# Writing out batch 0's TensorE queue by hand in a fused attention and SwiGLU kernel on one Trainium2 core

## The chip, the cores and the metric

The kernel runs on one core of one Trainium2 chip. The time is the device time of one execution in microseconds; with one core, this core's time is the kernel's. Times of a version are given as the median of its runs.

## What is computed

Attention over 8 batches of 12 heads, 448 positions and 64 numbers a head, and then a SwiGLU feed-forward block on the 3584 tokens. The weights are 768 x 1536 (gate and value) and 1536 x 768 (out).

```
scores = scale * np.matmul(q, k.transpose(0, 1, 3, 2))
attn = exp(scores - max) / (sum(exp) + 1e-9)
attn_out = np.matmul(attn, v)                     # (8, 12, 448, 64)
x = attn_out.transpose(0, 2, 1, 3).reshape(3584, 768)
g = x @ w_gate
silu = g * (1.0 / (1.0 + np.exp(-g)))
return (silu * (x @ w_val)) @ w_out               # (3584, 768), float32
```

## The kernel before

**Units of work.** Heads are worked in pairs: 48 pairs, 6 to a batch. Pairs below 12 (`QUAD`), the first two batches, keep their keys in chunks of 112, four to a pair. A *score tile* is one chunk of keys against all 448 queries of both heads: two matmuls into a tile of two PSUM banks (`qk`, line 287), followed by one exponential on ScalarE into `E` (line 301). `pv_chunk` (line 311) multiplies one chunk of `E` by V: eight matmuls of 65 columns into an accumulator, where column 64 gathers the sum of the exponentials. The fourth chunk is followed on VectorE by the reciprocal `R` and the product `xt` (lines 338 to 345). Pairs from 12 on use chunks of 128 keys, with a fourth, half chunk of two neighbouring pairs packed in one tile (`qk_quad`, line 257); their PV product is `pv_quad` (line 405), closed by `R` and `xt` for each head (lines 397 and 398).

**Turning.** Scores need q and k with the head's 64 numbers on the partitions (`qkT`). `prep` (line 199) makes them: pair 0 by matmuls with an identity (`turn0`), pairs 1 to 10 by TensorE transposes followed by one VectorE copy (`turn`, lines 243 to 253), pairs from 11 on by a reordering copy on POOL and a transposing DMA from SP (lines 188 to 197 and 211 to 221). The results `xt` are turned into `X`, the input of the feed-forward block, by `turn_x` (line 417): for pairs below 12 three matmuls and a VectorE cast (`X`, line 434), later by DMA. `turn_rests` (line 445) turns the last 64 queries of a batch's six pairs together.

**Feed-forward.** `ffn1_steps` (line 460) has 12 blocks of 128 hidden units. For each: a gate group of six matmuls into `gp`, a tanh on ScalarE (`sg`, line 480), a value group of six matmuls into `vp`, and two products on VectorE (`t`, line 484, and `hts`, line 487). `ffn2_steps` (line 492) multiplies the hidden units by `wo` in groups of 12 matmuls (`op`, line 510). In the first half-batch block a gate or value matmul has 384 columns.

**PSUM.** Two pools share the eight banks: `ps_s` has three tiles of two banks, given in rotation to score tiles, the early transposes and the gate groups; `ps_f` has two tiles of one bank, for accumulators, value groups, `op` and the other transposes.

**Order of the work.** Each engine works through its own queue in the order in which the program issues. Loads go through POOL's queue, in the order of the calls, except pair 0's; `load_v` brings V into `vraw`, and `copy_v` (line 167) copies it on VectorE into the tile `vo` that PV reads. `emit` issues the loads listed in `wq` when the score loop reaches a pair's second chunk. Batch 0 is the loop of lines 655 to 677: one score tile a turn, and between them, by conditions on the turn's number, the transposes of the coming pairs (`prep`), the V copies (`CAT`), the turned results (`XAT`), a few `dummy` matmuls and one or two PV chunks. From line 711 on a planner goes through `plan`: each visit `x` has two or three score tiles, and perhaps one or two pairs whose PV is due. A visit issues scores, the V copies for the next visit's pairs, loads and preps, PV, turned results, and then as many feed-forward steps as its budget allows. Visit 0 has the scores (6,0) and (6,1), the rest of batch 0's PV, the last two turned results and the first two feed-forward blocks.

The visit's head in the kernel before is this:

```
quads = [u for u in chunks if u[0] >= QUAD and u[1] == RU]
for pr, c in quads + [u for u in chunks if u not in quads]:
    qk(pr, c)
...
for p0 in vcopies.get(x, []):
    copy_v(p0)
```

Of the kernel before, what the change touches and what calls it, by code (L numbers as in the profile page):

```python
# [10 lines left out]
FP32 = mybir.dt.float32  # L11
FP16 = mybir.dt.float16
# [10 lines left out]
FIRST = 6  # L23
# [14 lines left out]
def kernel(  # L38
# [45 lines left out]
    xp = ctx.enter_context(tc.tile_pool(name="xp", bufs=2))  # L84
    hp_ = ctx.enter_context(tc.tile_pool(name="hp", bufs=2))
    fp = ctx.enter_context(tc.tile_pool(name="fp", bufs=3))
    ps_s = ctx.enter_context(tc.tile_pool(name="ps_s", bufs=3, space=PSUM))
    ps_f = ctx.enter_context(tc.tile_pool(name="ps_f", bufs=2, space=PSUM))

    Ebuf = [consts.tile([128, (NC * EB + 1) * D], FP16, name=f"E{i}") for i in range(NE)]  # L90
# [15 lines left out]

    wo = [consts.tile([128, NFB, OH], FP16, name=f"wo{i}") for i in range(2)]

    raw = {}
    qkT = {}  # L110
    X = {}

    def dummy(n):
        wp = ps_f.tile([128, 512], FP32, tag="f", name="wp")
# [84 lines left out]
    def prep(pr):  # L199
# [23 lines left out]

        def turn0():
            for t in range(2):
                tp = ps_s.tile([128, 2, 512], FP32, tag="s", name="tp")
                for c in range(NC):
                    for hx in range(2):
                        nc.tensor.matmul(
                            tp[ts(hx, 64), c // 2, ds(c % 2 * P, P)],  # L230
                            lhsT=qk16[:, 1 - t, c, hx],
                            rhs=ident[0:P, 0:P],
                            start=True,
                            stop=True,
                        )
                dst = qkT[pr][:, ts(1 - t, S)].rearrange("p (a x) -> p a x", a=2)
                nc.vector.tensor_copy(dst[:, 0], tp[:, 0, 0 : 2 * P])
                nc.scalar.activation(dst[:, 1], tp[:, 1, 0 : 2 * P], AF.Copy)
                if t == 0:
                    tq = tp  # L240
            nc.vector.tensor_copy(qkT[pr][:, 2 * S :], tq[:, 0, 0:D])

        def turn():
            if pr < FIRST + 2:
                tp = ps_s.tile([128, 2, 1024], FP16, tag="s", name="tp")[:, 0]
            else:
                tp = ps_f.tile([128, 1024], FP16, tag="f", name="tp")
            for i in range(2 * NC + 1):
                t, c = (1 - i // NC, i % NC) if i < 2 * NC else (0, 0)
                for hx in range(2):  # L250
                    src = raw[pr][t][:, hx, c, :]
                    nc.tensor.transpose(tp[ts(hx, 64), ts(i, P)], src, ident[0:P, 0:P])  # L252
            nc.vector.tensor_copy(qkT[pr][:], tp[:, 0 : 2 * S + D])
# [1 line left out]
        return turn if pr else turn0  # L255

    def qk_quad(pr, c):
        s = ps_s.tile([128, 2, 512], FP32, tag="s")
        if c < KR:
            t = qkT[pr]  # L260
            for hx in range(2):
# [25 lines left out]
    def qk(pr, c):  # L287
        if pr >= QUAD:
            return qk_quad(pr, c)
        t = qkT[pr]  # L290
        s = ps_s.tile([128, 2, 512], FP32, tag="s")
        for hx in range(2):
            nc.tensor.matmul(  # L293
                s[:, hx, 0:S],
                lhsT=t[ts(hx, 64), c * P : c * P + 128],
                rhs=t[ts(hx, 64), ds(S + (1 - hx) * D, S)],
                start=True,
                stop=True,
            )
        e = Es[pr % NE][:, ds(c * EB, 16)].rearrange("p (h b) x -> p h (b x)", h=2)  # L300
        nc.scalar.activation(e[:, :, 0:S], s[0:P, :, 0:S], AF.Exp, scale=sm_scale)  # L301
# [65 lines left out]
    def pv_open(pr):  # L367
        if pr not in accs:
            if wide(pr):
                acc = ps_s.tile([128, 2, 512], FP32, tag="s", name="acc")  # L370
                accs[pr] = ([acc[:, 0], acc[:, 1]], [0, 0], acc)
            else:
                accs[pr] = ([ps_f.tile([128, 512], FP32, tag="f", name="acc"), ps_f.tile([128, 512], FP32, tag="f", name="acc")], [0, 0])
# [69 lines left out]
        )  # L443

    def turn_rests(b):
        tp = ps_f.tile([128, NHP, D], FP32, tag="f", name="rtp")
        for p in range(NHP):
            for hx in range(2):
                nc.tensor.matmul(  # L449
# [7 lines left out]

    gate_small = [False]

    def ffn1_steps(kk, c0, n, hts):  # L460
        for fb in range(NFB):

            def group(kind, dst):
# [6 lines left out]
                        stop=(cb == NCB - 1),  # L470
                    )

            if gate_small[0]:
                gate_small[0] = False
                gp = ps_f.tile([128, 512], FP32, tag="f", name="gp")
            else:
                gp = ps_s.tile([128, 2, 512], FP32, tag="s", name="gp")[:, 0]
            group("g", gp)
            sg = fp.tile([128, 512], FP32, tag="sg")
            nc.scalar.activation(sg[:, 0:n], gp[:, 0:n], AF.Tanh, scale=0.5)  # L480
            vp = ps_f.tile([128, 512], FP32, tag="f", name="vp")
            group("v", vp)
            t1 = fp.tile([128, 512], FP32, tag="t1")
            nc.vector.scalar_tensor_tensor(  # L484
                t1[:, 0:n], sg[:, 0:n], 1.0, gp[:, 0:n], ALU.add, ALU.mult
# [1 line left out]
            nc.vector.scalar_tensor_tensor(  # L487
                hts[:, fb, 0:n], t1[:, 0:n], 0.5 * HS, vp[:, 0:n], ALU.mult, ALU.mult
            )
            yield  # L490

    def ffn2_steps(kk, c0, n, hts, first, last_block):
# [46 lines left out]
    def block(i):  # L539
        kk, odd = divmod(i, 2)  # L540
        c0, n = (384, 512) if odd else (0, 384)
        hts = hp_.tile([128, NFB, 512], FP16, tag="h")
        return ffn1_steps(kk, c0, n, hts), ffn2_steps(kk, c0, n, hts, i == 0, i == B - 1), n

    with tc.manual_schedule():
        load_qk32(0)
# [16 lines left out]
        dummy(7)  # L563
        prep(0)()
        dummy(1)
        turn = prep(1)

        wq = {
            0: [("qk", 6), ("g", 0), ("v", 0)],
# [75 lines left out]
        def share(total, at, n):  # L645
            return (at + 1) * total // n - at * total // n

        XAT = (11, 15, 17, 21)
        CAT = (4, 7, 11, 14, 17, 21)
        pieces = [(p, c) for p in range(FIRST) for c in range(NC)]  # L650

        def piece():
            pv_chunk(*pieces.pop(0))

        for u in range(FIRST * NC):
            pr, c = divmod(u, NC)
            qk(pr, c)
            if u == 1:
                dummy(1)
                turn()  # L660
                dummy(1)
            elif u == 3:
                dummy(2)
            elif u == 4:
                prep(2)()
            elif u >= 6 and c == 2:
                prep(pr + 2)()
            if c == 1:
                for w in wq.pop(pr, []):
                    emit(w)  # L670
            if u in CAT:
                copy_v(CAT.index(u))
            if u in XAT:
                turn_x(XAT.index(u))
            for _ in range(2 if c == 3 else int(c != 2 or u > 12)):
                if u >= 5 and pieces[0][0] * NC + pieces[0][1] <= u - 3:
                    piece()

        queue = []
        units = [divmod(x, NC) for x in range(QUAD * NC)]  # L680
# [30 lines left out]
        for x, (chunks, todo) in enumerate(plan):  # L711
            quads = [u for u in chunks if u[0] >= QUAD and u[1] == RU]
            for pr, c in quads + [u for u in chunks if u not in quads]:
                qk(pr, c)
            for _, p0 in todo:
                if p0 >= QUAD:
                    pv_piece(p0, RU)
            end = min([y for y in adds if y > x] + [len(plan) + 1])
            if x == 0:
                turn_x(4)  # L720
                while pieces:
                    piece()
                turn_x(5)
                add_block(0, end)
            for p0 in vcopies.get(x, []):
                copy_v(p0)
            entered = [pr for pr, c in chunks if c == 0]
            for pr in entered:
# [13 lines left out]
            for _, p0 in todo:  # L742
# [2 lines left out]
                    turns.append(p0)  # L745
                else:
                    turn_x(p0)
            for pr in entered:
                for w in wq.pop(pr, []):
                    emit(w)  # L750
            bare = not todo and bool(chunks)
            if adds[max(y for y in adds if y <= x)] < 2:
                if bare and oq and not fvq:
                    carry -= run_o()
# [60 lines left out]
```

The softmax here doesn't subtract the row's maximum and nothing guards it: scores larger than these inputs give would overflow.

## Time and profile before

| what | value |
| --- | --- |
| median of 5 runs | 452.09 us (450.84 to 452.89) |
| the profiled execution | 453.08 us, its span 451.3 us |
| TensorE matmuls busy | 439.3 us (97%) |
| TensorE weight loads busy | 247.1 us (55%) |
| ScalarE busy | 224.8 us (50%) |
| VectorE busy | 200.2 us (44%) |
| POOL busy | 180.2 us (40%) |
| gate and value matmuls (line 465) | 124.7 and 124.6 us |
| `op` matmuls (line 510) | 117.1 us |

PE stands for TensorE's matmuls, PEld for its weight loads, DVE for VectorE, ACT for ScalarE, POOL for GpSimd, SP for SyncE, whose queue issues the transposing DMAs. A line of the timeline gives start and duration in us, engine and line of the code, the operation with what it writes and reads, the shapes, and how many instructions are merged; in brackets the idle time before it and what ended it. Matmul ends are modelled and may overlap the next start. A line of the chain gives start, duration and what the time is put down to. A line of the windows view gives the stretch, its length, the busy time of PE, PEld, DVE, ACT and POOL, and last the granted share of TensorE's clock, the share of the DMA engines and GB/s.

### The profile page before, as it was taken

To read this page: it belongs to the slowest core of one execution; us is meant where nothing else is said; L and a number is where in the kernel's file an instruction comes from. 1 tells how busy PE (TensorE), PEld (TensorE's weight loads), DVE (VectorE), ACT (ScalarE), POOL (GpSimd) and SP (SyncE) were. 2 spreads that over 40 slices of the span, in tenths; PEclk is the share of its full clock that TensorE was granted. 3 is DMA by queue.
4 is the path that set the end of the run, shared out by engine and by line. 5 is a ranking of instruction groups with operands and counts; after the bars stand their busy time and mean duration, and the time that the engine had idled before them with its cause. 6 is when DMAs were issued, how large, how long until landed. Compare 5 with 4: busy or idle time off the path is not lost.

```text
span 451.3 us, 9959 instructions
## 1 busy us (share of the span) xinstructions
PE 439.3 (97%) x4024; PEld 247.1 (55%) x4024; DVE 200.2 (44%) x447; ACT 224.8 (50%) x332; POOL 180.2 (40%) x299
## 2 busy tenths in 40 slices
PE   7999999899999999999999999999999999999996
PEld 3656565444456556554556656554455656644464
DVE  4666563255565345344454535334544434045400
ACT  6965666456554555465536364455463651222222
POOL 8755716997775464335553267423000000000000
PEclk9999999899999999999999999999999999999999
DMA  9999999999997799984896687965131211200033
GB/s 143 176 200 201 198 179 148 151 219 159 130 137 89 116 140 125 143 102 66 110 122 104 107 136 99 152 78 103 32 78 47 48 45 22 77 30 1 0 107 105
DMA packets 108494, 49.90 MB, mean 111 GB/s; under 512 B 60832, under 2 KB 104992, under 8 KB 108448
## 3 DMA queue, kind: packets, MB, share of 16 engines
q0 software_dynamic: 46832, 24.56, 48.0%
q1 hardware_dynamic: 61520, 24.66, 29.4%
q8 instruction: 31, 0.51, 0.5%
q14 instruction: 15, 0.12, 0.1%
q10 hardware_dynamic: 96, 0.05, 0.0%
HBM read 49.55 MB, written 11.01 MB: 134 GB/s over the span
## 4 chain that ended last, share of the span: by engine, by line
PE 76%; DMA 12%; POOL 4%; DVE 3%; issue 2%; ACT 1%; DVEq 0%; POOLq 0%
PE op L510 23%; PE gp L465 22%; PE vp L465 19%; PE acc L356 8%; DMA k<-in_k_dram 5%; DMA wv<-in_moe_w_val_dram 4%; PE s L262 4%; DMA wg<-in_moe_w_gate_dram 2%; DVE t L484 1%; DVE hts L487 1%; ACT sg L480 1%; DMA vraw<-in_v_dram 1%; PE s L275 1%; POOL q L151 1%; POOL k L151 1%
## 5 line engine op out<-in xcount | busy, mean ns | idle before, releaser
L465 PE MATMUL gp<-X,wg 128*128 128x384 f16 (+1 forms) x576 | 124.7, 353 | 0.0
L465 PE MATMUL vp<-X,wv 128*128 128x384 f16 (+1 forms) x576 | 124.6, 352 | 0.0
L510 PE MATMUL op<-wo,hts 128*128 128x384 f16 (+1 forms) x684 | 117.1, 326 | 2.0 <-DVE xt L398 2.0
L283 ACT ACTIVATE E<-s 128x896 f16<-128x896 f32 x126 | 106.5, 922 | 14.4 <-PE s L262 9.2
L484 DVE SCALAR_TENSOR_TENSOR t<-sg,gp 128x384 f32<-128x384 f32 (+1 forms) x96 | 59.6, 621 | 119.5 <-ACT sg L480 119.5
L480 ACT ACTIVATE sg<-gp 128x384 f32<-128x384 f32 (+1 forms) x96 | 52.6, 548 | 92.9 <-PE gp L465 91.4
L510 PEld LDWEIGHTS <-hts 128*128 128x128 f16 x684 | 66.4, 99 | 48.2 <-issue 3.9
L465 PEld LDWEIGHTS <-wv 128*128 128x128 f16 x576 | 56.4, 98 | 52.6
L517 ACT ACTIVATE osb<-op 128x384 f32<-128x384 f32 (+1 forms) x57 | 27.6, 485 | 105.1 <-PE op L510 101.2
L465 PEld LDWEIGHTS <-wg 128*128 128x128 f16 x576 | 53.4, 98 | 45.5 <-issue 0.7
L487 DVE SCALAR_TENSOR_TENSOR hts<-t,vp 128x384 f16<-128x384 f32 (+1 forms) x96 | 59.6, 621 | 10.8 <-PE rtp L449 0.5
L188 POOL COPY qk<-k 128x512 f16<-128x512 f16 x36 | 22.8, 634 | 101.2 <-DMA qkT<-qk 99.1
L132 POOL DMA_DIRECT2D vraw<-in_v_dram x72 | 43.9, 631 | 14.6 <-DMA wo<-in_moe_w_out_dram 13.6
L356 PE MATMUL acc<-vo,E 128*128 128x65 f16 (+1 forms) x1152 | 43.1, 193 | 1.7 <-DVE hts L487 1.2
L301 ACT ACTIVATE E<-s 112x896 f16<-112x896 f32 x48 | 40.6, 916 | 7.9 <-PE s L293 7.8
L356 PEld LDWEIGHTS <-E 128*128 128x128 f16 (+1 forms) x1152 | 37.2, 96 | 13.1 <-issue 7.3
L132 POOL DMA_DIRECT2D k<-in_k_dram x70 | 42.4, 618 | 1.5 <-DMA wv<-in_moe_w_val_dram 0.8
L397 DVE RECIPROCAL R<-acc 128x4 f32<-128x4 f32 x68 | 12.1, 177 | 62.9 <-PE acc L356 62.9
L151 POOL DMA_DIRECT2D q<-in_q_dram x44 | 29.9, 680 | 4.8 <-PE tp L252 1.8
L398 DVE TENSOR_TENSOR xt<-acc,R 128x256 f16<-128x256 f32 x68 | 28.9, 424 | 2.3
L262 PE MATMUL s<-qkT 64*128 64x448 f16 x216 | 27.9, 353 | 0.0
L188 POOL COPY qk<-q 112x512 f16<-112x512 f16 x36 | 23.0, 640 | 0.0
(56 smaller groups left out, 184.4 us busy)
## 6 DMA issues: line engine op xcount, KB each, us to landing
vraw<-in_v_dram POOLq DMA_DIRECT2D x72, 64.0 KB, 4.7
q<-in_q_dram POOLq DMA_DIRECT2D x41, 112.0 KB, 3.6
k<-in_k_dram POOLq DMA_DIRECT2D x68, 64.0 KB, 4.5
wg<-in_moe_w_gate_dram POOLq DMA_DIRECT2D x8, 288.0 KB, 9.6
wv<-in_moe_w_val_dram POOLq DMA_DIRECT2D x8, 288.0 KB, 10.1
wo<-in_moe_w_out_dram POOLq DMA_DIRECT2D x2, 1152.0 KB, 19.9
out_dram<-osb SPq DMA_DIRECT2D x8, 288.0 KB, 4.1
out_dram<-osb SPq DMA_DIRECT2D x6, 336.0 KB, 2.9
```

Source lines behind the costliest of these rows:

```text
L132: eng.dma_start(dst[ts(s, 64)], rows)
L151: nc.gpsimd.dma_start(dst[0:P, ds(h0, 2 * n)], flat.rearrange("h (p c) d -> p h (c d)", c=NC))
L188: nc.gpsimd.tensor_copy(dst.rearrange("p c h d -> p h c d"), src)
L262: nc.tensor.matmul(s[:, hx, 0:S], lhsT=t[ts(hx, 64), ts(c + low(pr, hx), 128)], rhs=t[ts(hx, 64), ds(NC * 128, S)], start=True, stop=True,)
L283: nc.scalar.activation(e[:, 0 : 2 * S].rearrange("p (h q) -> p h q", h=2), s[:, :, 0:S], AF.Exp, scale=sm_scale)
L301: nc.scalar.activation(e[:, :, 0:S], s[0:P, :, 0:S], AF.Exp, scale=sm_scale)
L356: nc.tensor.matmul(accs[pr][0][hx][:, ts(j, D + 1)], lhsT=e[rows, ds(hx * S + j * 128, 128)], rhs=Vts[pr % NV][rows, hx, col, 0 : D + 1], ...
L465: nc.tensor.matmul(dst[:, 0:n], lhsT=wslice(kind, fb, cb), rhs=X[kk][:, cb, ds(c0, n)], start=(cb == 0), stop=(cb == NCB - 1),)
L480: nc.scalar.activation(sg[:, 0:n], gp[:, 0:n], AF.Tanh, scale=0.5)
L484: nc.vector.scalar_tensor_tensor(t1[:, 0:n], sg[:, 0:n], 1.0, gp[:, 0:n], ALU.add, ALU.mult)
L487: nc.vector.scalar_tensor_tensor(hts[:, fb, 0:n], t1[:, 0:n], 0.5 * HS, vp[:, 0:n], ALU.mult, ALU.mult)
L510: nc.tensor.matmul(op[:, 0:w], lhsT=hts[:, fb, ts(ch, 128)], rhs=wo[oh][:, fb, ds(m0 - oh * OH, w)], start=(fb == 0), stop=(fb == NFB - 1),)
```

## The change

Batch 0's loop is replaced by a list of items that are issued one by one: `s` a score tile, `t` a `prep`, `d` dummies, `v` a V copy, `p` a PV chunk, `x` a turned result, `b` one begun matmul. Score tiles often stand two in a row. Pair 1's transposes come right after score 0 and pair 2's after score 2.

The pool of score tiles becomes three fixed tiles (`sbanks`) and a ring of their numbers (`sring`): `stile` takes the oldest. `begin(n)` issues the n-th of the 24 gate and value matmuls of the first two feed-forward blocks. It takes a tile out of the ring at the first matmul of a block (b0 and b10) and keeps gate and value in its two banks; b20 to b23 are the four matmuls that need the last pair's `X`. In `ffn1_steps` these two blocks then have only tanh and the two products left, after which their tile goes back to the ring.

Scores 24 and 25 of the list are visit 0's, so visit 0 issues none. Also, a visit copies V for pairs from 12 on after its PV and turned results, not before; and batch 1's `turn_rests` takes a score tile in place of one of `ps_f`.

```diff
+    sbanks = [ps_s.tile([128, 2, 512], FP32, name=f"s{i}") for i in range(3)]
+    sring = [0, 1, 2]
...
+    def stile():
+        sring.append(sring.pop(0))
+        return sbanks[sring[-1]]
...
                 if t == 0:
-                    tq = tp
-            nc.vector.tensor_copy(qkT[pr][:, 2 * S :], tq[:, 0, 0:D])
+                    nc.vector.tensor_copy(qkT[pr][:, 2 * S :], tp[:, 0, 0:D])
...
+    def begin(n):
+        if n < 4 * (NCB - 1):
+            fb, r = divmod(n, 2 * (NCB - 1))
+            j, cb = divmod(r, NCB - 1)
+        else:
+            (fb, j), cb = divmod(n - 4 * (NCB - 1), 2), NCB - 1
+        if fb == len(begun):
+            begun.append(sring.pop(0))
+        nc.tensor.matmul(
+            sbanks[begun[fb]][:, j, 0:MQ],
+            lhsT=wslice("gv"[j], fb, cb),
+            rhs=X[0][:, cb, 0:MQ],
+            start=(cb == 0),
+            stop=(cb == NCB - 1),
+        )
...
+            if fb < ahead:
+                gp, vp = sbanks[begun[fb]][:, 0], sbanks[begun[fb]][:, 1]
...
+            if fb < ahead:
+                sring.append(begun[fb])
...
+        order = """
+            s0 t1 s1 d1 s2 t2 s3 d2 s4 v0 s5 p0 p1 t3 s6 v1 p2 p3 s7 t4 s8 x0 p4 s9 s10 p5 v2 p6 p7 s11 s12 p8 p9
+            x1 t5 v3 s13 p10 p11 s14 s15 p12 p13 s16 x2 t6 v4 s17 p14 p15 s18 s19 p16 p17 t7 s20 x3 p18 s21 v5 s22
+            p19 b0 b1 b2 b3 p20 p21 x4 s23 s24 p22 b4 b5 b6 b7 b8 p23 s25 b9 b10 b11 b12 b13 x5
+            b14 b15 b16 b17 b18 b19 b20 b21 b22 b23
+        """
...
-                qk(pr, c)
+                if x > 0:
+                    qk(pr, c)
...
-            for p0 in vcopies.get(x, []):
+            early = [p0 for p0 in vcopies.get(x, []) if p0 < QUAD]
+            for p0 in early:
                 copy_v(p0)
...
+            for p0 in vcopies.get(x, []):
+                if p0 not in early:
+                    copy_v(p0)
```

## The prediction

> **What bounds the kernel now.** I read the page, then the chain that ended last, then the timeline engine by engine where they disagree. By the page, TensorE is busy for 97% of the span, but the chain up to 82 us isn't made of TensorE work. It runs over DMAs, POOL and VectorE:
>
> ```profile
> 51.32 20.45 DMA k<-in_k_dram
> ...
> 72.55 1.17 POOL qk L188 x2
> ...
> 76.06 5.59 DMA vraw<-in_v_dram
> ...
> 81.75 0.40 DVE vo L169
> 82.15 0.10 DVE R L397
> ...
> 82.27 0.43 DVE xt L398
> ...
> 82.75 5.67 PE op L510 x24
> ```
>
> A transfer of keys ordered at 51 us lands at 71.8, POOL reorders them (72.55), the next V lands at 81.65, VectorE copies it, and only then does TensorE's `op` start. From there the chain is almost all TensorE. So two stretches matter: batch 0, before about 33 us, which the change rewrites, and the join with the DMA chain at 79 to 83 us, which lies behind it. The timeline of the join, TensorE first and then VectorE:
>
> ```profile
> 78.64 0.38 PE L449 MATMUL rtp<-ident,xt 128*64 128x64 f16 x12 [0.41 <-ACT osb L517]
> 78.95 0.74 PE L262 MATMUL s<-qkT 64*128 64x448 f16 x6
> 79.53 1.25 PE L356 MATMUL acc<-vo,E 64*128 64x65 f16 x32
> 82.75 5.67 PE L510 MATMUL op<-wo,hts 128*128 128x384 f16 x24 [1.97 <-DVE xt L398]
> ...
> 81.75 0.40 DVE L169 COPY vo<-vraw 128x512 f16<-128x512 f16 x1 [2.13 <-DMA vraw<-in_v_dram]
> 82.07 0.17 DVE L397 RECIPROCAL R<-acc 128x4 f32<-128x4 f32 x1
> 82.27 0.42 DVE L398 TENSOR_TENSOR xt<-acc,R 128x256 f16<-128x256 f32 x1
> ```
>
> The PV product of pair 12 ends at 80.78. Its reciprocal could start, but ahead of it in VectorE's queue stands the copy of pair 13's V, whose transfer hasn't landed; TensorE's next matmuls need the accumulator and idle 1.97 us. Then the 24 `op` matmuls take 5.67 us, where 24 of them took 4.06 at 67.28. The windows view says why:
>
> ```profile
> 80.00:90.00 10.00, 8.03 (x88) 4.68 (x87) 2.30 (x7) 3.92 (x7) 9.68 (x18) 0.83 1.49 152
> ```
>
> The granted clock there is 0.83, in the windows beside it 1.00: some 3.4 us of half clock, which cost 5.67 - 4.0 = 1.7 us. This place costs 1.97 + 1.7 = 3.65 us together.
>
> In batch 0, ScalarE is what is full:
>
> ```profile
> 6.16 5.03 ACT L301 ACTIVATE E<-s 112x896 f16<-112x896 f32 x6 [0.30 <-PE s L293]
> 11.39 8.39 ACT L301 ACTIVATE E<-s 112x896 f16<-112x896 f32 x10 [0.19 <-PE s L293]
> 19.98 2.53 ACT L301 ACTIVATE E<-s 112x896 f16<-112x896 f32 x3 [0.20 <-PE s L293]
> 22.72 6.08 ACT L301 ACTIVATE E<-s 112x896 f16<-112x896 f32 x7 [0.21 <-PE s L293]
> ```
>
> 26 exponentials in 22.64 us, 22.03 of it busy, 0.84 us apart; TensorE's queue has gaps of 0.65 us (10.0) and 0.96 us (28.1) and is otherwise closely filled.
>
> **What the Trainium skill says.** *TensorE: Matmul & The Clock Gate*, "What's actually happening": TensorE's clock is halved after too little activity in a free-running window of about 3.4 us. The trace agrees on the length (0.17 x 10 us x 2 = 3.4 us) and shows that 1.97 us of idling among small matmuls sufficed, while 0.96 us at 28.1 left the clock at 1.00. *Perfetto Trace Analysis*, "Tensor Engine Instruction": VectorE and ScalarE work strictly in order; the reciprocal waiting behind the copy is that. *DMA: Bandwidth & Descriptors*, "Issuing engines are not separate DMA queues": POOL's and SP's transfers share the same DMA engines. The trace agrees: the `qkT` transposes land 10 to 13 us after issue beside `wo` (54 to 59 us) and 4.5 us after it at 74.47.
>
> **What TensorE can't move.** POOL's waits from 16 to 72 us end with landings of earlier transfers (13.6 us of them with `wo`). Where the view names TensorE instead (18.18, 26.53, 40.15), the buffer had long been free and the issue simply follows the wait by 0.54 us. So I take these landings as fixed, from issue plus time to landing: `wo` 63.2 and 71.0; `qkT` of pair 12 66.2, of 13 71.9, of 14 79.0 (74.47 + 4.5), of 15 84.9 (78.62 + 6.3); V of 13 81.65, of 14 85.8.
>
> **The change, part by part, batch 0.** A lone score tile costs 0.30 us to the next item and 0.11 more than eight PV matmuls (0.24) after them; one more in the same run costs 0.225 (three take 0.75). So each of the 6 pairs saves 0.82 - 0.64 = 0.18, 1.1 us in all, and one dummy (0.22) goes. Against this, pair 2's transposes are moved ahead of score 3, and its keys land at 8.1 (3.97 + 4.2): TensorE waits some 0.5 us, and exponential 6 starts at about 11.75 instead of 11.39. From there ScalarE paces at 0.84: exponential 21 ends at 25.2, 22 at 26.0, 25 at about 29. The 24 begun matmuls (24 x 0.1625 = 3.9 us) add no work, they lie in TensorE's slack beside ScalarE. Scores 23 and 24 have only two tiles left and wait for exponentials 21 and 22 (26.05); value 0's second half lands at 26.0, just ahead of its use. Then p22, b4 to b8, p23 to 27.75, score 25, b9 to b13 to 28.95, pair 5's normalisation to 28.9, x5, its copy until 29.9 beside b14 to b19, and the last four matmuls to 30.75. Before, the four groups end at 33.2: 2.4 us are won.
>
> Some is given back. Score (6,3) takes the tile held for block 0, free only after tanh (30.45 + 0.49) and the two products (to 32.15): TensorE stands 1.2 us, no tile being left to hide it. Block 2's gate then starts at about 33.1 (before 34.30), PV of pair 6 at 36.1 (37.69). **Batch 0 is worth about 1.6 us** (bounds 0 to 2.5); further on nothing waits for a DMA up to pair 13's scores (72.6, landed 71.9).
>
> The rest: the explicit score ring in place of the pool rotates the same way: nothing. Copying the tail of `qkT` earlier on VectorE (0.23 us) changes the order of three operations with the same sum: nothing, and 0.23 at the worst, which the join would swallow. The second `turn_rests` in a score tile saves the 0.41 us at 78.23; the third score of that visit then waits for its 0.56 us cast, under the wait named next.
>
> **The join.** TensorE reaches it 1.6 + 0.4 = 2.0 us earlier, at 76.95. Two scores later comes (14,0), whose `qkT` lands at 79.0: it stands 1.6 us, until 79.05, where before it ran at 79.33. So nearly all of batch 0's gain is lost here; 0.25 is left. PV of 12 runs from 79.3 to 80.5. Now the V copy stands behind the reciprocal and the product, not ahead. At 214.7, where nothing is in the way, the first head's accumulator is free 0.48 us after the last PV matmul is issued (214.85 to 215.33): `op` starts at 81.05 instead of 82.75, **1.7 us**. At full clock it ends at 84.95 (24 x 0.1625), when pair 15's keys land as well; before, the scores there start at 88.36: **3.35 us** gained, 1.65 of it clock. The moved copy itself waits for 81.65, ends at 82.1, and PV of 13 wants it at 85.7. In later visits the copy (0.3 to 0.7 us) falls between the second product's end (215.87) and the next operation (216.98): hidden, and up to 0.15 us a visit if not. SP and POOL see the same order as before. After 83 us TensorE waits only 0.2 us at a time, so the gain stays to the end.
>
> Sum: the profiled execution took 453.08 (span 451.27 and 1.81 around it); 453.08 - 3.35 = 449.7. It lies 0.99 above the median of 452.09, so 448.74 there; I take off 0.25 of the gain, since TensorE meets two landings without cover: **449.0**.
>
> **Rivals.**
> 1. *The stall moves and halves the clock again* (28%): the new 1.6 us at 77.4 plus 0.45 at 80.5 come to the same idle time as the 1.97. Or the median run before had no half clock to lose. Against it: dense `op` matmuls lie before the one and after the other. Gain 3.35 - 1.65 - 0.25 = 1.45: 450.6.
> 2. *The DMA chain moves forward with TensorE* (8%): then batch 0's gain comes on top, 3.35 + 1.6 - 0.25 = 4.7: 447.4. Against it: POOL's 13.6 us on `wo`.
> 3. *The V copy wasn't what held `op`* (6%), or pair 15's keys land some 3 us later under the denser traffic: only 0.3 is left, 451.8.
> 4. *Slower* (6%): the moved V copies push the `hts` products in each of some 34 visits, and TensorE, which waits for `hts` 0.2 us in 6 visits already, waits longer. At 0.15 us a visit, 5.1 - 3.1 = 2.0 lost: 454.1. It decides from 0.09 us a visit. Against it: the 1.1 us of slack on VectorE.
>
> The forecast itself has 52%, with its own range 448.2 to 449.8. About 0.3% (1.36 us) can be told from no change. Faster than 450.7: all of the first, two thirds of rival 1, rival 2: 0.79; the same 0.15; slower 0.06. The range 447.8 to 451.0 reaches to rival 1 and leaves out 2, 3 and 4.
>
> **What would show it.** Block 0's tanh at about 30.5; an idle stretch of some 1.2 us ahead of score (6,3) at 32; PV of 6 at 36; a TensorE wait for `qkT` ending near 79.05; `op` at 81.05; scores at 85; granted clock 1.00 from 80 to 90. Wrong if `qkT` of 14 lands before 78, if the clock is halved there again, or if `acc` waits grow after 90 us.

## Result and the profile after

| | kernel before | kernel after |
| --- | --- | --- |
| median | 452.33 us (450.21 to 455.85, 71 runs) | 452.76 us (450.61 to 454.88, 36 runs) |
| profiled execution | 453.08, span 451.3 | 451.15, span 449.4 |
| granted clock in it | 0.996 | 1.00 |

The ratio after to before is 0.9996 with an interval of 0.9983 to 1.0009: no difference that can be measured. The forecast was 449.0.

The profiled execution after is 1.93 us shorter than the one before, and still the medians are the same. So the profiles of one execution each don't answer the question alone. The record has the span and the granted clock of every run, and span times (1 - clock) is the time that half clock cost in it. Over all runs these costs lie below 0.5, at 1.8 to 2.3 or at 3.6 to 4.1 us: none, one or two stretches of 3.4 us at half clock, which cost half their length. (Nine runs lie at 0.9. One of them is profiled, and there the half clock lies in the thinning work after 447.5 us, at the kernel's end.) I count a run as having such a stretch where the cost is at least 1.3 us:

| kernel | runs | with a stretch | median without | with one | with two |
| --- | --- | --- | --- | --- | --- |
| before (beside the experiments) | 207 | 64 (31%) | 451.9 to 452.0 | 453.8 to 454.1 | 455.6 to 456.0 |
| after | 36 | 25 (69%) | 451.15 | 453.04 | 454.23 |

(The ranges of the first row are those of three groups of runs, of 57, 75 and 75.) The kernel after is 0.8 us faster where the clock stays full, and loses this by having the stretch more than twice as often. The profile before, on which the forecast stood, showed one of the 31%; the profile after shows one of the 31% of its kernel that have none.

The chain that ended last, of the kernel after, the part that answers to the one shown before (start, duration, what the time is put down to):

```profile
51.51 20.21 DMA k<-in_k_dram
...
72.30 1.19 POOL qk L194 x2
...
74.22 5.86 DMA qkT<-qk
...
80.22 0.37 PE s L267 x2
80.58 0.61 PE acc L361 x20
...
81.21 0.19 DVE R L402
...
81.43 0.43 DVE xt L403
...
81.91 4.07 PE op L543 x24
```

The chain is the same up to POOL's reordering at 72.3: a TensorE that is earlier hasn't moved the DMAs. Then it parts. Before, it went through V of pair 13 and its copy on VectorE; now it goes through the transposes of pair 14, which land at 80.08, and reaches TensorE there. `op` starts at 81.91 instead of 82.75.

TensorE's timeline at the join, kernel after:

```profile
77.03 0.55 PE L267 MATMUL s<-qkT 64*128 64x448 f16 x4
80.22 0.37 PE L267 MATMUL s<-qkT 64*128 64x448 f16 x2 [2.63 <-DMA qkT<-qk]
80.40 1.14 PE L361 MATMUL acc<-vo,E 64*128 64x65 f16 x32
81.91 4.07 PE L543 MATMUL op<-wo,hts 128*128 128x384 f16 x24 [0.37 <-DVE xt L403]
85.91 0.38 PE L280 MATMUL s<-qkT 64*64 64x448 f16 x4
```

TensorE comes to the first two scores of the visit at 77.03, as forecast (76.95), and stands 2.63 us for the third, which belongs to pair 14. From the end of PV to `op` it now waits 0.37 us instead of 1.97: the V copy is out of the way. And in this execution the 24 `op` matmuls took 4.07 us, so the clock was full:

```profile
80.00:90.00 10.00, 9.41 (x110) 5.73 (x111) 3.84 (x10) 4.93 (x7) 10.00 (x18) 1.00 1.67 154
```

Batch 0 in TensorE's timeline, kernel after:

```profile
30.57 0.36 PE L298 MATMUL s<-qkT 64*128 64x448 f16 x2
32.07 0.37 PE L298 MATMUL s<-qkT 64*128 64x448 f16 x2 [1.14 <-DVE hts L518]
...
32.93 1.15 PE L492 MATMUL gp<-X,wg 128*128 128x384 f16 x6
...
36.05 0.36 PE L324 MATMUL acc<-vo,E 112*128 112x65 f16 x6
```

The last line is PV of pair 6; in the kernel before it is this:

```profile
37.69 0.34 PE L319 MATMUL acc<-vo,E 112*128 112x65 f16 x6 [0.21 <-DVE hts L487]
```

It starts at 36.05 instead of 37.69: 1.64 us ahead. The first `op` of the kernel, at 65.84 (before 67.28), still has 1.44 of it.

### The profile page after: what moved, and what is told of

Its sections match the earlier page's. It is cut to its first block, busy times and chain, and to the rows that moved or that the text cites. A ratio compares the mean times of both kernels' runs of the same rounds, so it can differ in the third digit from the quotient of the medians.

```text
span 449.4 us, 10030 instructions
## 1 busy us (share of the span) xinstructions
PE 436.4 (97%) x4023; PEld 245.8 (55%) x4023; DVE 198.4 (44%) x447; ACT 224.8 (50%) x332; POOL 180.1 (40%) x299
## 4 chain that ended last, share of the span: by engine, by line
PE 78%; DMA 14%; DVE 3%; POOL 2%; issue 1%; ACT 1%; SPq 0%; DVEq 0%; ACTq 0%; POOLq 0%
PE op L543 23%; PE s L492 21%; PE vp L492 19%; PE acc L361 8%; DMA k<-in_k_dram 6%; DMA q<-in_q_dram 5%; PE s L267 4%; DMA wg<-in_moe_w_gate_dram 2%; DVE hts L518 1%; DMA qkT<-qk 1%; DVE t L515 1%; ACT sg L510 1%; PE s L280 1%; POOL q L157 1%; PE s L298 0%
## 5 line engine op out<-in xcount | busy, mean ns | idle before, releaser
L492 PE MATMUL vp<-X,wv 128*128 128x512 f16 (+1 forms) x564 | 122.4, 353 | 0.0
L492 PE MATMUL s<-X,wg 128*128 128x512 f16 (+1 forms) x540 | 117.5, 354 | 0.0
L543 PE MATMUL op<-wo,hts 128*128 128x384 f16 (+1 forms) x684 | 115.5, 323 | 0.4 <-DVE xt L403 0.4
L515 DVE SCALAR_TENSOR_TENSOR t<-sg,s 128x384 f32<-128x384 f32 (+1 forms) x92 | 57.2, 622 | 107.9 <-ACT sg L510 107.9
L510 ACT ACTIVATE sg<-s 128x384 f32<-128x384 f32 (+1 forms) x92 | 50.4, 549 | 93.5 <-PE s L492 91.1
L492 PEld LDWEIGHTS <-wv 128*128 128x128 f16 x564 | 55.2, 98 | 51.8
L492 PEld LDWEIGHTS <-wg 128*128 128x128 f16 x564 | 52.3, 98 | 44.9 <-issue 0.7
L518 DVE SCALAR_TENSOR_TENSOR hts<-t,vp 128x512 f16<-128x512 f32 (+1 forms) x94 | 58.5, 622 | 10.1 <-DVE t L515 0.5
L361 PE MATMUL acc<-vo,E 128*128 128x65 f16 (+1 forms) x1088 | 40.8, 193 | 2.2 <-DVE hts L518 1.9
```

Of the source, the lines that this page charges most:

```text
L361: nc.tensor.matmul(accs[pr][0][hx][:, ts(j, D + 1)], lhsT=e[rows, ds(hx * S + j * 128, 128)], rhs=Vts[pr % NV][rows, hx, col, 0 : D + 1], ...
L492: nc.tensor.matmul(dst[:, 0:n], lhsT=wslice(kind, fb, cb), rhs=X[kk][:, cb, ds(c0, n)], start=(cb == 0), stop=(cb == NCB - 1),)
L515: nc.vector.scalar_tensor_tensor(t1[:, 0:n], sg[:, 0:n], 1.0, gp[:, 0:n], ALU.add, ALU.mult)
L518: nc.vector.scalar_tensor_tensor(hts[:, fb, 0:n], t1[:, 0:n], 0.5 * HS, vp[:, 0:n], ALU.mult, ALU.mult)
L543: nc.tensor.matmul(op[:, 0:w], lhsT=hts[:, fb, ts(ch, 128)], rhs=wo[oh][:, fb, ds(m0 - oh * OH, w)], start=(fb == 0), stop=(fb == NFB - 1),)
```

## Experiments

Four questions stood open: which part of the change carries which sign; whether the 2.63 us wait is what halves the clock; whether the wait can be taken away at its source; and what the ring of score tiles costs. My theory was that the DMA landings pace everything up to about 86 us, that the late V copies are a gain by themselves, and that batch 0's lead only becomes a wait, behind which the clock is halved. The rivals were that the rewrite of batch 0 or its ring costs time further on, and that the half clock has nothing to do with the wait.

### The late V copies alone

The kernel before, with nothing but the two places of the V copy.

```diff
+            early = [p0 for p0 in vcopies.get(x, []) if p0 < QUAD]
-            for p0 in vcopies.get(x, []):
+            for p0 in early:
                 copy_v(p0)
...
+            for p0 in vcopies.get(x, []):
+                if p0 not in early:
+                    copy_v(p0)
```

> The kernel before with one part of the change alone: V copies for pairs from 12 on stand behind PV. If the DMA chain holds TensorE at score (14,0) (theory A), this part carries what the change wins at the join: score (14,0) at about 79.3 to 80 us as before, op at 81 to 82 instead of 82.75, so 0.8 to 1.5 us less than before in span times clock, and the time as good as that of the whole change. If it is the rewritten batch 0 that wins or loses (theory B), this run is within 0.3 us of before.

Measured: 451.31 us (450.01 to 452.04, 22 runs), ratio 0.9967 (0.9952 to 0.9982), and in none of the 22 runs a stretch of half clock. The expectation that this part alone carries the gain came true; without a stretch the kernel before beside it takes 451.98 us, so the gain there is 0.7 us, a little under the 0.8 to 1.5 expected. TensorE at the join:

```profile
79.54 0.84 PE L262 MATMUL s<-qkT 64*128 64x448 f16 x6
80.20 1.17 PE L356 MATMUL acc<-vo,E 64*128 64x65 f16 x32
81.73 4.08 PE L510 MATMUL op<-wo,hts 128*128 128x384 f16 x24 [0.37 <-DVE xt L398]
86.43 0.38 PE L275 MATMUL s<-qkT 64*64 64x448 f16 x3 [0.32 <-DMA qkT<-qk]
```

With the old batch 0 TensorE comes to these scores at 79.54, and the first three run through with no wait for pair 14 that the view lists; its keys land at 79.9 here. `op` starts at 81.73, even before that of the kernel after (81.91). On VectorE the reason can be seen:

```profile
81.25 0.42 DVE L398 TENSOR_TENSOR xt<-acc,R 128x256 f16<-128x256 f32 x1
...
82.93 0.29 DVE L169 COPY vo<-vraw 128x512 f16<-128x512 f16 x1 [0.70 <-DMA vraw<-in_v_dram]
```

The product comes first, and the copy waits for its V behind it, where nobody wants it yet. From the scores behind `op` to the end this kernel takes as long as the kernel before (362.9 us each), so the later visits lose nothing by it. The next experiment shows that the rest of the change, alone, gains nothing in the median.

### Batch 0's rewrite alone

The kernel after, with all V copies back in their old place.

```diff
-            early = [p0 for p0 in vcopies.get(x, []) if p0 < QUAD]
+            early = list(vcopies.get(x, []))
```

> The changed kernel with the V copies put back ahead of PV, so batch 0's rewrite alone. Theory A: TensorE arrives at score (14,0) some 1.5 us early, stands there until qkT of pair 14 lands near 79 to 80, and op then waits for the V copy until about 82.7: no gain against before, and 0.3 us lost to later tanh operations. Theory B: it keeps 1 us or more of batch 0's lead of 1.4 us.

Measured: 454.58 us (451.50 to 456.11, 12 runs), ratio 1.0044 (1.002 to 1.0068), so slower by 0.4%. 10 of the 12 runs have two stretches of half clock; the other two took 451.50 and 452.49.

```profile
81.70 0.36 PE L267 MATMUL s<-qkT 64*128 64x448 f16 x2 [2.54 <-DMA qkT<-qk]
81.89 1.59 PE L361 MATMUL acc<-vo,E 64*128 64x65 f16 x32
```

```profile
83.50 0.46 DVE L175 COPY vo<-vraw 128x512 f16<-128x512 f16 x1 [4.08 <-DMA vraw<-in_v_dram]
```

```profile
80.00:90.00 10.00, 7.21 (x54) 4.20 (x55) 2.19 (x6) 2.14 (x3) 9.27 (x17) 0.66 1.54 149
```

The new wait of 2.54 us comes first, then the old one behind the V copy, which still costs `op` 1.09 us. The windows view gives 0.66 for these 10 us: 0.34 x 2 x 10 = 6.8 us at half clock. So the two parts of the change have opposite signs, and together they come to nothing.

### Is it the wait that halves the clock?

The kernel after, with ten matmuls of zeros on TensorE in the place of the wait; they change nothing in what is computed.

```diff
             for pr, c in quads + [u for u in chunks if u not in quads]:
+                if (pr, c) == (14, 0):
+                    dummy(10)
```

> The changed kernel with ten 512-column matmuls of zeros (2.15 us) in the queue just ahead of (14,0), in the time in which TensorE waits there anyway. Theory C (the clock halves because of this wait, which adds 1.7 us in most runs): no run with a half clock, time without half clock still about 451.0, median 451.0 to 451.4 instead of 452.8. If the half clock comes from elsewhere (batch 0 or the wait at 31 us): as often as in the changed kernel, median 452.5 to 453.

Measured: 452.21 us (450.90 to 455.04, 22 runs), ratio 0.9999 (0.9984 to 1.0014). Runs with a stretch of half clock: 2 of 22, against 25 of 36.

```profile
77.91 2.33 PE L122 MATMUL wp<-warm 128*128 128x512 f16 x10
80.17 0.36 PE L267 MATMUL s<-qkT 64*128 64x448 f16 x2
...
81.86 4.07 PE L543 MATMUL op<-wo,hts 128*128 128x384 f16 x24 [0.37 <-DVE xt L403]
```

The gap is filled, everything else stands where it stood, and the half clock is all but gone. So it is this wait that brings it. The time missed its expectation all the same: the 20 runs without a stretch have a median of 452.14, against 451.15 of the kernel after without one. Two reasons can be named. The ten matmuls hold TensorE for some 2.2 us whether or not the keys are there: in this profile the keys land at 79.7 and TensorE comes to them at 80.17. And a batch 0 that is late for its own reasons (1.5 us in some profiles, see the last experiment) has no wait left to be swallowed in. How much of the 1.0 us each makes isn't shown.

The traces also show why one wait halves the clock in some executions and not in others. They record each change of TensorE's granted clock. From the first full clock to the start of the half clock it is 78.507 us in the profile before, 75.093, 81.920 and 129.706 in three others: 23, 22, 24 and 38 times 3.413 us, the length of one stretch. So the changes lie on a grid of 3.413 us, whose place in the program differs from execution to execution. Laid over the matmul records, this grid gives TensorE's idle time in each of its windows. These are the windows with a wait over 1.5 us, and whether the clock is halved when they end:

| profile | window, us | TensorE idle in it, us | clock after it |
| --- | --- | --- | --- |
| before | 79.21 to 82.63 | 1.85 | half |
| output groups first, pool, later load, more dummies | 131.47 to 134.88 | 2.40 | half |
| batch 0's rewrite alone | 78.91 to 82.32 | 2.54 | half |
| output groups first, pool | 83.15 to 86.57 | 2.56 | half |
| after with pool tiles | 77.37 to 80.79 | 3.27 | half |
| after | 75.53 to 78.94, then to 82.35 | 1.35, then 1.65 | full |
| after, later `wo` | 75.79 to 79.21 | 1.73 | full |
| before, later `wo` | 76.18 to 79.60 | 1.72 | full |
| output groups first, pool, later load | 128.66 to 132.07, then to 135.49 | 1.38, then 0.87 | full |

(Most of these kernels follow below.) From the first full clock to the kernel's end no window of the 14 profiles breaks the order. With 1.85 us of idling or more in one window half clock follows, with 1.76 or less the clock stays full; the 1.76 is at the end of a kernel, where TensorE runs out of work. Once the clock is half, a window with 1.0 to 1.1 us of idling keeps it so (batch 0's rewrite alone and the fourth of the table, which have two windows of half clock), and one with at most 0.12 ends it. The wait of 2.63 us in the profile after was spared because an edge of the grid, at 78.94, cut it in two.

### Taking the wait away at its source

The second transpose of pair 14 landed 5.9 us after its issue in the profile after, and POOL's queue ahead of it is held up by the weights. So I ordered `wo`'s second half two pairs later, in the kernel after and in the one before.

```diff
-            7: [("o", 1)],
+            9: [("o", 1)],
```

> The changed kernel with the second half of wo loaded after pair 15's q and k and pair 12's V, not before. Theory A: pair 14's keys and its qkT land at 72 to 76 us instead of 80, score (14,0) no longer waits, op starts at about 79.5 instead of 81.9, and the kernel ends 2 to 2.6 us earlier than the changed one, unless the op matmuls of wo's second half (74.5) now wait for its landing. Theory B: no change, since the wait for qkT only stands in for another loss.

> The kernel before with the same move of the load. Theory A: pair 13's V lands several us earlier, op no longer waits 1.97 us and the half clock behind it goes: span times clock 1.5 to 2 us below before, and the run with both (the changed kernel with this load order) below this one by batch 0's 1.4 us less 0.3. Theory B: as before.

Measured: 453.31 us (451.24 to 454.94, 22 runs), ratio 1.0001 (0.9983 to 1.0019), a stretch in 13 of 22; and for the kernel before 451.93 us (451.02 to 452.80, 14 runs), ratio 0.9992 (0.9976 to 1.0007), a stretch in none of 14. Both gains failed to come; the first expectation had named what could spoil it. TensorE with the change:

```profile
77.52 2.12 PE L543 MATMUL op<-wo,hts 128*128 128x384 f16 x12 [2.10 <-DMA wo<-in_moe_w_out_dram]
```

The keys of pair 14 do land 2 us sooner, at 78.11, but the wait has only changed its transfer: now the `op` matmuls ahead of them want the second half of `wo`, which lands at 77.48. In the kernel before it is the same:

```profile
77.98 2.12 PE L510 MATMUL op<-wo,hts 128*128 128x384 f16 x12 [1.72 <-DMA wo<-in_moe_w_out_dram]
```

### Other work ahead of the wait

The other way is to give TensorE work that it has: the 24 `op` matmuls of this visit right after its first score, ahead of the one that waits. In the kernel after, and in the first experiment's.

```diff
                 if x > 0:
                     qk(pr, c)
+                if x == 11 and budget is None:
+                    budget = left() / (end - x) + carry
+                    budget -= run_o()
+                    budget -= run_o()
...
-                carry = run_budget(left() / (end - x) + carry)
+                carry = run_budget(left() / (end - x) + carry if budget is None else budget)
```

> The changed kernel with the two output groups of visit 11 (24 op matmuls, 3.9 us, which need nothing of pair 14) issued after that visit's first score, ahead of (14,0). Theory A (batch 0's lead is real, and is lost in the wait for qkT of pair 14): the stall of 2.6 us is covered, no half clock there, time without half clock about 448.8 instead of 451.0, median the same 448.8 to 449.2. Theory B (the lead is lost elsewhere): within 0.5 us of 451.

> The kernel before with late V copies and the same two output groups ahead. TensorE has no lead to lose here and hardly waits for qkT of pair 14. Theory A: within 0.6 us of the run with late V copies alone (451.3), so that the difference to the changed kernel with the same move is batch 0's lead, 1.4 us less 0.3. Theory B: as low as the changed kernel with this move.

Measured: 451.21 us (449.88 to 455.26, 22 runs), ratio 0.9982 (0.9963 to 1.0001), a stretch in 7 of 22; and without the rewrite of batch 0 451.74 us (450.50 to 456.59, 22 runs), ratio 0.9991 (0.9973 to 1.0008), in 2 of 22. The kernel after with it:

```profile
78.83 4.07 PE L543 MATMUL op<-wo,hts 128*128 128x384 f16 x24
...
85.38 0.38 PE L280 MATMUL s<-qkT 64*64 64x448 f16 x3 [0.47 <-DMA qkT<-qk]
```

The wait for pair 14 is gone. But TensorE now reaches pair 15's keys sooner, and these land at 85.33. The median without a stretch fell only from 451.15 to 451.02, not to the 448.8 expected. In this profile TensorE's full clock came only at 10.6 us and put batch 0 1.5 us behind, so the wait was short; the profile of the next experiment shows it in full. Where there is no lead (451.74 against 451.31) the move has nothing to win. Between the two kernels with the move, which differ by batch 0's rewrite, 0.5 us are left of the 1.1 that the lead should be worth, and their intervals overlap.

### The ring of score tiles

The kernel after, with the score tiles taken from the rotating pool again once visit 0 is over; then the same together with the `op` move. (The lines left out give the pool its three buffers back and take the ring's tiles from it.)

```diff
     def stile():
+        if pooled[0]:
+            return ps_s.tile([128, 2, 512], FP32, tag="s", name="s")
         sring.append(sring.pop(0))
...
         for x, (chunks, todo) in enumerate(plan):
+            pooled[0] = x > 0
```

> The changed kernel, with the score tiles taken from the rotating pool again once visit 0 is over, so that the ring of fixed tiles serves batch 0 alone. In the trace a tanh starts 1.56 us after its gate group with the ring and 1.50 with the pool. If the ring does that: tanh at 1.50, the PV waits for hts at 0.20 instead of 0.26 us, time without half clock 0.3 to 0.6 us below the changed kernel's 451.0; half clocks as often as there. If the late V copies do it: no difference.

> The changed kernel with visit 11's two output groups ahead of (14,0) and with pool tiles after visit 0. The wait for qkT of pair 14 is covered, but the run with the output groups alone stood 0.47 us for qkT of pair 15 at 84.9 us. Theory A (the DMA chain sets the pace up to 86 us, one transfer after the other): the next transposes land at 85.4, so at most 0.5 us below the run with late V copies alone (451.3): 450.8. Theory B (TensorE's lead comes through as soon as one wait is covered): 449.5.

Measured: 451.82 us (450.40 to 454.31, 22 runs), ratio 0.9985 (0.9969 to 1.0002), a stretch in 13 of 22; and with the `op` move 451.63 us (449.42 to 455.32, 22 runs), ratio 0.9988 (0.9965 to 1.0011), in 11 of 22. What the ring costs can be read in the feed-forward blocks. The kernel after, one gate group, its tanh and the PV after it:

```profile
208.15 1.46 PE L492 MATMUL s<-X,wg 128*128 128x512 f16 x6
...
209.71 0.60 ACT L510 ACTIVATE sg<-s 128x512 f32<-128x512 f32 x1 [0.86 <-PE s L492]
...
211.87 1.12 PE L361 MATMUL acc<-vo,E 64*128 64x65 f16 x31 [0.27 <-DVE hts L518]
```

and with the pool:

```profile
209.51 1.46 PE L496 MATMUL s<-X,wg 128*128 128x512 f16 x6
...
211.01 0.60 ACT L514 ACTIVATE sg<-s 128x512 f32<-128x512 f32 x1 [0.80 <-PE s L496]
```

From the gate's start to the tanh it is 1.56 us with the ring, 1.50 with the pool and before. In both the tanh waits for two semaphores, and one of the two waits has an instruction of its own ahead of it. With the ring this is TensorE's, the one that comes late: it is met at 209.64, and the tanh starts at 209.71. With the pool it is one that was met 1.3 us before. The 0.06 us show on TensorE where PV waits for `hts`, 0.26 us against 0.20 in six places from 42 to 317 us. Counted at these PV products, the kernel after is 2.44 us ahead of the profile before at 94 us and 1.90 at 317, while the late V copies alone stay 1.93 ahead from 94 to 317. With the pool the lead stands still up to 160 us and then falls by 0.35 at once, at 213.5, where one wait for `hts` is 0.56 us long. So the pool takes away the small losses and brings another one, and the 0.3 to 0.6 us expected can't be seen in the time: 451.18 us without a stretch, against 451.15. With the `op` move and the pool the eleven runs without a stretch have a median of 450.27, the lowest of all kernels here. The profiled one was not among them; its largest wait and the windows after it:

```profile
PE s L284 <- DMA qkT<-qk: 3.6, 1, 3.6
```

```profile
80.00:90.00 10.00, 6.36 (x81) 3.83 (x79) 1.32 (x5) 4.33 (x7) 9.07 (x17) 0.83 1.59 143
90.00:100.00 10.00, 9.80 (x80) 4.72 (x78) 5.14 (x13) 4.34 (x6) 9.25 (x16) 0.83 1.12 205
```

TensorE stands 3.6 us here in front of pair 15, and the clock is halved for 2 x 0.17 x 2 x 10 = 6.8 us. That is more than batch 0's lead: these keys landed at 87.5, 2.2 us later than in the experiment before.

### A load less ahead of pair 15

Pair 16's q and k are loaded one visit later, together with pair 17's, so that the transposes of 14 and 15 share the DMA engines with less: on top of the last kernel, and on top of the late V copies alone.

```diff
-if 14 <= pr + LA < NPAIR:
+if 14 <= pr + LA < NPAIR and pr != 10:
+    if pr == 11:
+        load_qk16(pr + LA - 1, 1)
     load_qk16(pr + LA, 1)
```

> The same, with pair 16's q and k loaded with pair 17's, one visit later, so that 240 KB less stand beside the transposes of pairs 14 and 15. Theory A: qkT of pair 15 lands 1 to 2 us earlier than 85.4, (14,RU) starts at 83.5 to 84.5, and 0.8 to 1.5 us of the lead come through: 449.5 to 450.2. Theory B: no difference to the run without it.

> The kernel before with late V copies and the same later load of pair 16. TensorE has no lead here: theory A gives at most the 0.3 us for which it stood for qkT of pair 15 at 86.1: 451.0 against 451.3. A gain as large as in the changed kernel would speak against batch 0's lead as its source.

Measured: 450.73 us (449.38 to 453.73, 22 runs), ratio 0.9962 (0.9942 to 0.9982), a stretch in 4 of 22; and without batch 0's rewrite 450.67 us (450.02 to 452.24, 22 runs), ratio 0.9961 (0.9946 to 0.9977), in none of 22. The second transpose of pair 14 now lands 3.4 us after its issue in the one and 3.8 in the other, against 4.5 to 5.9 in the kernels that order their transfers as before. In the first, pair 14 is there at 78.48 and pair 15 at 83.41, and TensorE waits for neither. Its largest waits then are these:

```profile
PE s L496 <- DMA X<-xt: 2.2, 1, 2.2
...
PE acc L365 <- DVE vo L179: 0.4, 1, 0.4
```

The lead goes on to 131 us and is lost there, in front of the next DMA transposes (`X`). The first expectation, 449.5 to 450.2, was missed. Without a stretch the first kernel is no faster than the one it builds on (450.67 against 450.27); what it gains in the median comes from fewer stretches, 4 of 22 against 11. The second kernel has no lead to lose and ends at the same median, 0.64 us below the late V copies alone, where 0.3 were expected. They were measured in different groups of runs, but the kernel before took the same in both groups (451.98 and 451.94 without a stretch). By the test set beforehand this speaks against batch 0's lead as the source of the first kernel's gain; where the second one's comes from stays open. These two are the fastest here.

### TensorE's clock at the start

In three of the profiles (batch 0's rewrite alone, the `op` move, and the late V copies with the later load) TensorE's clock became full only at 10.4 to 10.6 us instead of 3.8 to 5.8, and batch 0 was 1.5 us later. It shows in the matmuls: two of a score tile take 0.55 us before and 0.36 after. The runs' granted clock doesn't show it; the windows view too gives 1.00 for the first 10 us of these three. I put more of the list's dummies among its first scores, in the kernel with the `op` move, the pool and the later load, to see whether thin work at the start does that.

```diff
-            s0 t1 s1 d1 s2 t2 s3 d2 s4 v0
+            s0 d1 t1 s1 d1 s2 d2 t2 s3 d2 s4 v0
```

> The kernel with output groups first, pool tiles and pair 16's later load, and three more 512-column dummy matmuls in the first 8 us, in times in which TensorE waits for pair 1's and pair 2's loads. In two of six profiles of the rewritten batch 0 the clock stayed halved until 10.6 us, in none of the four of the old one, and batch 0 was 1.5 us later. If the thinner start does that: full clock by 6 us in the profile, and the slow half of the run's times (1 us above the fast half) goes, median 0.3 to 0.7 us lower. If not: no difference.

Measured: 451.08 us (449.98 to 454.04, 23 runs), ratio 0.9965 (0.9951 to 0.998), a stretch in 1 of 23. There is no gain in time, so the cure isn't one. Its profile has the full clock at 5.2 us, as expected, but so have most profiles without it, and one profile can't tell how often it comes late. What the 14 profiles do show is again the grid: in the three late ones its edges lie at 3.6 to 3.8, 7.0 to 7.2 and 10.4 to 10.6 us, and the clock became full at the third; in the other eleven the first edge after the first matmuls lies at 3.85 to 5.8, and the clock became full there. Why the window up to 7.2 us wasn't enough in the three stays open.

## Why the prediction was wrong

**The bound: right.** DMA landings pace the kernel up to about 86 us and don't follow TensorE. POOL's reordering of the keys that the chain names comes at 72.30 (before 72.55) although TensorE was 1.4 us ahead. Rival 2 falls. (One of POOL's waits, 1.18 us at 44.54, the view puts down to a V copy on VectorE; the prediction passed over it, and POOL came no later for it.)

**Batch 0: right.** 1.6 us were forecast, 1.64 measured in two profiles whose clock became full early (3.85 and 4.12 us); tanh of block 0 at 30.35 (30.5), the idle stretch ahead of score (6,3) 1.14 us (1.2), PV of pair 6 at 36.05 (36.1).

**The V copy: right in kind, half in size.** The wait of `op` fell from 1.97 to 0.37, as forecast. But `op` starts 0.84 us earlier, not 1.7, since pair 14's keys landed at 80.08, not at 79.0. I had taken 4.5 us from issue to landing out of a single profile and written it down as fixed. In the nine profiles whose kernels order these transfers alike it is 4.5 to 5.9 us, the issue lies at 74.2 to 76.3, and the landing at 79.0 to 81.6. The wait that I priced at 1.6 us became 2.6, and 1.9 us of lead at the join turned into a wait and nothing else.

**The clock: the step that failed.** "At full clock it ends at 84.95" counted 1.65 us of half clock as lost before and never after. Both halves of that are wrong. Before, 31% of the runs lose it, not all, though the profile shows it; the median run has nothing of it to give back. The sum then took off another 0.99 because the profiled execution lay above the median, but it lay there because of the half clock: the same time was taken off twice. From the median only the earlier `op` could come off: 452.09 - 1.7 = 450.4 by my own figure, and half of the 1.7 was there. After, 69% lose it, because the lead comes to stand as one wait, so the median run is one that pays. Three kernels show it from three sides: with the wait filled, 2 of 22 runs have a stretch; with the V copies late and no lead, 0 of 22; with the lead and the V copies early, 10 of 12, twice over. This was rival 1, in both of its readings at once, and its reason was right: the idle time is of the same size as before. A clock halved there again was also among the signs that I had written down for being wrong. I let myself be led away from it by the dense `op` matmuls around the new wait, and gave it 28%. What went with the half clock in all the profiles is the idle time within one window of 3.413 us, and that can't be seen from the work on either side of it. Rival 1's own 450.6 was too low, since the gain of 1.45 us that it left for the V copies was 0.8 even in runs with full clock on both sides, and it took the half clock after to be no more frequent than before.

**The rest: mostly right.** The late copies cost nothing in later visits, as the kernel with them alone shows. The ring was forecast at nothing; it costs 0.06 us at a tanh, and the kernel after loses 0.5 us of its lead between 94 and 317 us, most of it in places that the pool keeps clean. Rivals 3 and 4 didn't happen as told. The change does hold a slower kernel, but that is batch 0's rewrite alone (454.58), not the moved V copies.

**Where the gain went.** Of the 1.64 us in batch 0, 0.2 are gone by the first `op` and all of the rest at the join, in front of pair 14. With that wait covered by `op`, they are lost in front of pair 15; with that load moved, in front of `X` at 131 us. The 0.7 us that the late V copies earn are paid out again as half clock in the median run.

**What stays open:** why the kernel with the filled wait is 1.0 us slower than the one after where neither has half clock; why the later load wins 0.64 us without batch 0's lead; why the clock at the start needs a third window in some executions; whether an order of all loads up to 131 us would let batch 0's lead through. The last kernels with a later load stop short of that.

## What to carry to other kernels

Where a chain of transfers paces the work, time won ahead of it comes out as a wait, and the wait can cost more than it holds, since TensorE's clock may be halved behind it. So look first at the landing that comes next, or have other useful work ready to put in front of it, and speed up the work ahead of it only then. Ask of a stall in one profile how often the runs have it, before you count it as a gain; the span and granted clock of every run tell that. And don't take off the same loss twice, once as a cost in the profile and once as the profile's distance from the median. Last, in a queue that runs strictly in order, an operation that waits for a transfer goes behind those that don't, even where all are short: that alone was worth 0.33% here, with one copy moved.

## What the runs showed of the hardware

*TensorE: Matmul & The Clock Gate*, "What's actually happening", in the Trainium skill, says that TensorE's clock is halved after an idle window of about 3.4 us, and that these windows run free, not starting with the kernel. The traces agree on the length and on the free running: the half clock lasts 3.413 us or twice that, and its start lies a whole number of windows after the first full clock (23, 22, 24, 21 and 38 in five profiles), at another place of the program each time. They differ on "idle". A window needn't be idle throughout: 1.85 us of idling within one was enough and 1.76 was not, from the first full clock to the end in the 14 profiles here. So a wait of 2.63 us can pass, cut in two by an edge, where one of 1.97 us doesn't. How often the runs have the half clock doesn't follow from the length of one profile's wait alone: 1.97 us go with 31% of the runs and 2.63 us with 69%, but the waits of 2.2 and 2.8 us in front of `X` at 131 us with only 4 of 22 and 1 of 23. Why those are so few isn't shown.

An instruction on ScalarE whose late semaphore has a wait instruction of its own starts 0.06 us later than one that waits for the late one itself (1.56 us after the gate group's start against 1.50). The second DMA transpose of pair 14 took 4.5 to 5.9 us to land in nine profiles of nine kernels that order their transfers alike.
